# A fused attention and two-layer MoE kernel: another order of the same 2,222 pieces

## The chip, the cores and the metric

The kernel runs on one core of one Trainium2 chip. The time is the device time of one execution in microseconds (us); a kernel's time is the median of its runs. Engines are named as in the profile: PE (TensorE matmuls), PEld (TensorE's weight loads), DVE (VectorE), ACT (ScalarE), POOL (GpSimd) and SP (the queue that issues most DMAs).

## The reference

Three stages follow one another, all in float32:

```python
# attention: q is averaged over pairs of rows, then softmax(q k^T / 8) v
q_pool = q.reshape(B, H, S // 2, 2, D).mean(axis=3)      # B, H, S, D = 2, 8, 1152, 64
scores = np.matmul(q_pool, k.transpose(0, 1, 3, 2)) / np.sqrt(D)
attn = np.exp(scores - scores.max(-1, keepdims=True))
attn = attn / (attn.sum(-1, keepdims=True) + 1e-9)
x = np.matmul(attn, v)                                   # -> 1152 tokens x 512
# layer 1 (d_ff 1536)
g = x @ w_gate
x = (g / (1 + np.exp(-g)) * (x @ w_val)) @ w_out
# layer 2 (d_ff 2048)
h = x @ w_in
x = (np.maximum(h, 0) + alpha * np.minimum(h, 0)) @ w_out2
```

## The kernel before

**Pieces and tiles.** The program is built from 2,222 pieces. A piece is one instruction of DVE, ACT, POOL or SP, or a run of 2 to 20 matmuls on PE that write one PSUM bank. `add()` numbers the pieces as the code reaches them; each has an engine, a duration that the planner assumes, the tokens that it reads and writes, and the buffers that it uses. Some have two ways: the subtraction that makes the low half of a float32 operand (`lower`: L490 on DVE or L491 on POOL), the copy that makes the high half (`higher`: L498 on ACT or L499 on POOL), the sums of weight blocks (L537 on DVE or L536 on POOL), the evacuation of transposes (L765 on ACT or L766 on DVE), and a few more.

**Attention** goes over 8 pairs of heads. For each pair there are scores (L732, the upper and lower 64 rows of the array side by side, and L751 for a corner), row minima on DVE while the scores are copied out of PSUM (L700, L702), the exponential on ACT (L706), transposes on PE (L775, L789) with their evacuations (L765, L766), the product with v (L808, the array's columns side by side) and a rescaling. PE changes between whole array, half rows and half columns as the pieces ask.

**The layers** multiply each float32 operand as a high and a low half, in three matmuls. Token block 0 is multiplied directly (`contract`, L907, 12 matmuls of 384 columns). Token blocks 1 and 2 go through a seven-product (Strassen) scheme: `block` issues seven `seventh` pieces (L919, 6 matmuls each), whose sums are made on DVE from PSUM (`plus`, L925). Layer 1 then applies Silu on ACT (L975) and the gate product on DVE (L980), layer 2 its slopes (L1019, L1020); both split the result in two halves (L498 and L490, L966 and L967). The output products are `out1` (L1050, added up by L1055 and L1057) and `out2` (L1084, 12 matmuls of 512 columns, added up by L1090 and L1092, the last token block as two halves), and SP sends each finished row block out (L1094). Each pair of weight blocks is loaded by two DMAs into one of two raw buffers, unpacked by ACT and DVE (L517 to L520), summed (L536, L537) and split.

**Order.** Nothing reorders at run time. The string `ORDER` holds one code for each piece: twice its number, plus one if its second way is taken. `Plan.run` goes through the codes, gives each buffer a slot that is free by then, and the pieces are emitted in that order, so that each engine's queue is the codes of that engine in their order. An engine waits at the piece whose inputs or slots are not ready, and everything behind it on that engine waits too.

```python
        for code in codes:
            t = self.tasks[code // 2]
            w = t.way = t.ways[code % 2]
            e = w.eng
...
            for i, b in enumerate(t.bufs):
                if b.slot is None:
                    spots = [(room(s, at), k, s) for k, s in enumerate(self.classes[b.cls]["slots"])]
                    _, _, b.slot = min(x[:2] + (x[2],) for x in spots if x[0] is not None)
```

PSUM has eight banks. In the layers each PE piece takes one (class "b"); it is free again when the last piece that reads it, on DVE or ACT, is done. PE also gets short idle matmuls (L367) while it waits at the start, where the planner sees room.

Pieces that are named below, by code: 2492 is `out1` of output block 3, token block 1, and its evacuation is L1055; 2632 is the `plus` behind a `seventh` (code 2630); 2202 is the `contract` of `value1(3)` and 2188 the `lower` piece of its weights; 2360 is the gate product of `value1(4)`; 2978 is an `out1` of the second group and 2980 its addition (L1057); 4420, 4432 and 4438 are the last `out2` pieces (row block 6 and the two halves of row block 8), with 4422, 4434 and 4440 as their additions and 4424, 4436 and 4442 as their stores.

Of the kernel before, what the change touches and what calls it, by code (L numbers as in the profile page):

```python
# [33 lines left out]
8 20 10 48 50 12 24 26 34 54 14 60 52 56 16 22 98 39 40 62 66 18 58 64 86 68 92 28 30 88 70 72 90 94 82 84 76 32 46 154 100 74 96 44 80 36 79 104 102 130  # L34
132 156 158 138 134 108 106 112 136 160 110 42 162 260 264 266 114 116 118 120 166 122 164 262 140 270 272 170 192 194 142 168 174 172 198 200 204 196 206
210 202 208 212 124 268 126 129 276 278 150 153 188 191 144 149 146 492 230 176 181 226 178 182 228 494 184 232 280 187 234 236 496 238 240 242 502 504 214
216 282 220 222 224 286 218 284 318 290 322 288 320 324 292 294 298 326 330 332 336 370 506 366 362 328 334 364 338 246 248 352 296 300 368 372 374 302 304
251 314 316 724 308 728 355 340 310 307 382 344 313 385 386 342 390 392 388 396 346 348 376 378 274 380 398 394 350 402 406 400 424 426 428 430 432 436 438
434 440 244 254 356 256 258 404 358 498 500 361 442 420 726 408 444 413 422 410 414 416 508 462 458 419 464 460 446 448 510 451 252 512 514 466 468 516 518
520 452 456 522 550 556 454 470 472 474 524 554 526 530 476 528 532 552 558 562 560 594 564 568 596 602 566 598 600 604 570 478 480 606 482 730 732 742 734  # L40
584 586 546 484 548 534 537 538 486 540 542 545 572 576 574 614 489 617 618 620 956 624 740 578 582 580 622 608 612 610 626 630 628 490 632 636 656 0 658
662 634 664 638 668 660 960 670 962 674 736 666 672 676 964 588 590 592 694 652 640 655 645 972 642 646 690 648 696 692 678 680 651 683 744 698 746 700 702
748 750 752 684 688 958 782 784 966 686 754 788 790 756 758 762 794 796 800 830 786 760 764 792 798 802 968 826 828 834 832 836 710 712 715 778 781 838 816
766 818 804 846 771 809 768 848 772 776 774 850 854 852 856 860 806 810 812 814 840 844 862 858 866 870 888 890 894 864 900 868 842 896 1184 1192 902 1194
1408 906 892 898 904 738 820 908 822 884 872 825 874 1412 704 887 877 878 706 708 883 880 922 924 910 912 926 928 976 915 974 1182 978 1186 1188 930 932
982 980 916 918 920 984 1014 1018 1016 986 988 990 994 1020 1024 1026 992 2 996 1190 1066 1022 1030 1034 1058 1060 716 1028 1032 1062 1064 1068 1070 942
944 947 1010 1013 1048 998 1050 1001 1004 1009 1002 1006 1078 1080 934 1036 1038 718 720 722 1082 1084 1086 1040 1088 1090 1042 1044 936 1072 1046 1076
1092 1074 1094 1126 1096 1098 1102 1120 1122 1132 1100 1128 1124 970 1052 1134 1138 1932 1130 1136 1414 1416 1424 1054 1140 1158 1057 1116 1119 1104 1109
1106 1198 1110 1154 1112 1200 1156 1115 1160 1142 1147 938 1144 940 1202 1204 1206 1162 1164 1148 1426 950 1240 1242 1244 1208 1150 1152 948 1210 1246 1934
1212 1214 1216 1936 1220 1248 1218 1222 1252 1254 1258 1292 1250 1256 1410 1260 1284 1286 1288 1290 1294 1296 1166 1168 1170 1174 1176 1179 1418 1938 1274  # L50
1236 1238 1276 1224 1228 1230 1670 1232 1196 1304 1227 1306 1262 1266 1308 1420 1310 1264 1234 1312 1172 1180 1314 1316 1318 1268 1674 1270 1272 1298 1302
1320 1322 1300 1324 1326 1346 1348 1350 1352 1328 1354 1358 1278 1280 1360 1364 1356 1362 1342 1330 1940 1366 1345 1335 1282 1332 1336 1380 1382 1338 1368
1370 1428 1384 1386 1388 1341 1390 1392 1394 1396 1373 1434 1398 1430 1432 1374 1376 1440 1436 1472 1438 1378 1442 1446 1676 1466 1672 1468 1478 1444 1448
1474 1470 1480 1514 1510 1512 1484 1476 1518 1482 1486 1516 1520 1522 1400 1402 1500 1404 1462 1464 1678 1450 1502 1452 1456 1942 1455 1460 952 1688 1422
1530 1459 1968 1948 1532 1488 1534 1492 1538 1490 1540 1524 1528 1494 1498 1536 1544 1542 1496 1546 1550 954 1554 1680 1682 1572 1574 1406 1548 1552 1576 4
1684 1578 1944 1526 1584 1580 1586 1504 1582 1506 1588 1590 1509 1568 1571 1592 1556 1559 1610 1612 1560 1562 1606 1608 1567 1690 1694 6 1970 1594 1564
1614 1616 1618 1696 1596 1692 1698 1598 1600 1602 1728 1700 1730 1702 1706 1734 1736 1946 1953 1704 1740 1972 1732 1604 1710 1686 1772 1955 1742 1776 1774
1708 1960 1738 1744 1724 1727 1950 1746 1957 1959 1718 1721 1712 1620 1748 1714 1780 1778 1782 1964 1962 1974 1722 1976 1762 1764 1716 1796 1798 1750 1753
1800 1754 1756 1758 1802 1804 1966 1897 1834 1760 1846 1840 1806 1784 1838 1844 1808 1898 1812 1816 1902 1635 1641 1642 1626 1836 1842 1850 1628 1854 1810
1637 1848 1978 1622 1630 1900 1624 1632 1814 1654 1852 1872 1650 1985 1653 1874 1766 1768 1770 1792 1830 1660 1795 1833 1818 1876 1823 1878 1824 1827 1820  # L60
1880 1868 1870 1980 1828 1882 1786 1788 1791 1856 1861 1858 1862 1866 1865 1988 1639 1982 1904 2012 1663 1644 1987 1664 1666 1646 1990 1888 1648 1656 1658
1992 1668 1890 1884 1886 1994 2004 1892 1894 2014 1916 1996 2024 1906 1922 1924 2030 2046 1918 1920 1912 1915 2006 1926 1908 2008 2010 1910 2050 2096 2016
2098 2100 2102 2104 2020 2106 1928 1931 2018 2054 2058 2048 2052 2108 2112 2022 2026 2028 2034 1998 2040 2068 2056 2036 2076 2110 2060 2114 2086 2168 2166
2170 2172 2062 2116 2118 2124 2132 2032 2070 2120 2122 2136 2174 2144 2042 2140 2176 2064 2128 2134 2066 2183 2000 2002 2150 2262 2260 2264 2266 2138 2078
2142 2154 2088 2178 2180 2185 2186 2146 2160 2188 2190 2192 2038 2080 2268 2082 2084 2044 2210 2332 2270 2272 2212 2214 2330 2216 2156 2334 2218 2090 2336
2280 2282 2092 2072 2074 2094 2152 2232 2234 2130 2202 2204 2220 2424 2222 2162 2206 2274 2278 2276 2224 2338 2284 2208 2286 2148 2226 2288 2426 2428 2296
2194 2250 2298 2240 2340 2228 2230 2300 2242 2158 2308 2342 2345 2304 2430 2314 2350 2352 2446 2432 2252 2346 2348 2302 2126 2196 2444 2244 2358 2434 2366
2306 2198 2292 2236 2354 2356 2440 2386 2442 2310 2200 2448 2246 2450 2164 2254 2316 2436 2452 2374 2376 2324 2396 2238 2256 2318 2294 2454 2456 2368 2378
2258 2382 2438 2502 2460 2462 2458 2248 2290 2360 2500 2504 2370 2372 2506 2508 2510 2517 2320 2312 2521 2472 2474 2322 2536 2380 2398 2384 2388 2512 2514
2496 2498 2582 2540 2326 2522 2584 2586 2676 2404 2588 2390 2519 2590 2328 2524 2526 2406 2468 2414 2592 2678 2408 2532 2680 2748 2682 2684 2392 2542 2548  # L70
2550 2528 2410 2416 2418 2362 2538 2552 2595 2394 2597 2601 2566 2556 2470 2476 2602 2604 2400 2544 2534 2402 2412 2598 2554 2558 2530 2606 2686 2608 2746
2750 2752 2560 2562 2840 2564 2570 2572 2464 2420 2568 2688 2690 2754 2756 2695 2576 2574 2693 2422 2610 2618 2478 2842 2696 2630 2698 2578 2546 2612 2701
2620 2622 2702 2364 2466 2614 2624 2860 2626 2628 2616 2762 2844 2488 2490 2758 2760 2764 2580 2632 2862 2492 2494 2480 2634 2482 2484 2638 2486 2636 2846
2648 2640 2848 2656 2666 2642 2650 2644 2658 2704 2652 2767 2770 2668 2646 2654 2708 2660 2706 2670 2662 2768 2672 2712 2664 2710 2864 2674 2716 2772 2714
2720 2850 2724 2866 2852 2888 2718 2856 2890 2730 2854 2858 2774 2868 2722 2732 2870 2782 2726 2872 2994 2776 2876 2996 2874 2734 2728 2878 2892 2740 2736
2894 2738 2790 2778 2742 2896 2744 2794 2792 2780 2798 2898 2998 2802 2784 3092 2900 2796 2908 2812 3094 2903 2904 2800 2880 2814 2906 2804 2910 2912 2820
2914 2830 2806 2882 2884 2822 3096 3000 2824 2832 2916 2886 2834 3002 2920 2918 3098 3004 3100 2924 3014 3112 3006 3114 2922 3009 3010 2928 2786 2926 2808
# [1111 lines left out]
```

## Time and profile before

| | before |
|---|---|
| runs, us | 601.98, 601.80, 602.91 (median 601.98) |
| the profiled execution: its own time, us | 601.89 |
| its span (first to last instruction), us | 600.1 |
| granted TensorE clock over the span | 1.000 |
| PE, PEld, DVE, ACT, POOL busy, share of the span | 99%, 88%, 86%, 61%, 29% |

The time of an execution holds the span and 1.8 us around it. Busy shares are unions of an engine's instructions; matmuls overlap, so that a busy PE need not be a PE at its best pace.

### The profile page before, as it was taken

The page shows a single profiled execution, that of the slowest core. Times are in us where ns is not written, and L with a number is a line of the kernel's source. Part 1 is how long each engine was busy: PE and PEld are TensorE (multiplying, and loading weights), DVE is VectorE, ACT ScalarE, POOL GpSimd, SP SyncE. Part 2 cuts the span into 40 slices and gives each one's busy share as a digit, 9 for nine tenths or more (in the row PEclk, how much of TensorE's full clock was granted, in tenths as well). Part 3 has the DMA queues.
Part 4 walks back from the last instruction along what each step waited for, and adds up shares of the span by engine and source line. Part 5 has one row for each costly group of instructions (what it writes and reads, how often), then busy time and mean ns, then how long its engine had stood idle before and what let it go on. Part 6 is the DMA issues. An engine that isn't in the chain of part 4 may idle for free.

```text
span 600.1 us, 12138 instructions
## 1 busy us (share of the span) xinstructions
PE 593.8 (99%) x4736; PEld 531.0 (88%) x4736; DVE 518.8 (86%) x1050; ACT 365.2 (61%) x626; POOL 171.7 (29%) x188
## 2 busy tenths in 40 slices
PE   8999999999999999999999999999999999999997
PEld 5877877877886999999999999999999989989986
DVE  6988988989898999999859999889999999988552
ACT  5898888998998556555436334346675654544320
POOL 5552536230754313111300300556110300320000
PEclk9999999999999999999999999999999999999999
DMA  5342143232300431432303323112113313110012
GB/s 160 128 131 69 52 161 112 101 101 76 137 22 21 174 108 71 141 140 89 123 0 141 126 89 138 71 70 71 71 70 107 129 46 141 70 71 0 1 64 95
DMA packets 17913, 55.35 MB, mean 92 GB/s; under 512 B 2808, under 2 KB 4288, under 8 KB 17856
## 3 DMA queue, kind: packets, MB, share of 16 engines
q1 hardware_dynamic: 17568, 54.19, 25.9%
q8 instruction: 37, 0.61, 0.4%
q10 hardware_dynamic: 288, 0.39, 0.2%
q14 instruction: 20, 0.16, 0.1%
HBM read 52.17 MB, written 2.40 MB: 91 GB/s over the span
## 4 chain that ended last, share of the span: by engine, by line
PE 98%; DVE 2%; issue 0%; DVEq 0%
PE bank L919 24%; PE bank L1084 16%; PE bank L907 14%; PE bank L1050 12%; PE bank L808 12%; PE bank L732 9%; PE bank L775 6%; PE bank L751 2%; PE bank L789 1%; PE bank L367 1%; DVE wide L702 0%; DVE turned L490 0%; DVE wide L700 0%; DVE weights L490 0%; PE bank L822 0%
## 5 line engine op out<-in xcount | busy, mean ns | idle before, releaser
L919 PE MATMUL bank<-fed,weights 128*128 128x384 f32 x600 | 114.2, 335 | 0.0
L536 POOL TENSOR_TENSOR magnitudes<-magnitudes 128x256 f32<-128x256 f32 x58 | 50.8, 888 | 193.1 <-DVE magnitudes L520 143.3
L919 PEld LDWEIGHTS bank<-fed,weights 128*128 128x128 f32 x600 | 105.4, 188 | 0.7
L1084 PE MATMUL bank<-wide,turned 128*128 128x512 f32 (+1 forms) x444 | 101.7, 384 | 0.0
L1084 PEld LDWEIGHTS bank<-wide,turned 128*128 128x128 f32 x444 | 81.5, 188 | 15.4
L907 PE MATMUL bank<-x,weights 128*128 128x384 f32 x480 | 88.7, 337 | 0.0
L907 PEld LDWEIGHTS bank<-x,weights 128*128 128x128 f32 x480 | 83.8, 188 | 1.7 <-issue 0.7
L706 ACT ACTIVATE wide<-wide,stats 128x1152 f32<-128x1152 f32 x60 | 74.9, 1251 | 13.6 <-DVE wide L702 13.3
L1050 PE MATMUL bank<-turned,wide 128*128 128x384 f32 x432 | 77.5, 335 | 0.6 <-DVE plain L925 0.6
L1050 PEld LDWEIGHTS bank<-turned,wide 128*128 128x128 f32 x432 | 75.1, 188 | 0.9 <-DVE plain L925 0.9
L702 DVE TENSOR_SCALAR_CACHE_REDUCE wide<-bank,stats 128x384 f32<-128x384 f32 x120 | 70.2, 614 | 3.7 <-DVE wide L702 0.6
L808 PE MATMUL bank<-turned,plain 128*64 128x320 f32 (+1 forms) x576 | 73.1, 408 | 0.0
L925 DVE TENSOR_TENSOR plain<-bank,plain 128x384 f32<-128x384 f32 x100 | 54.0, 549 | 16.8 <-PE bank L919 15.7
L765 ACT ACTIVATE turned<-bank 128x512 f32<-128x512 f32 (+2 forms) x130 | 62.7, 555 | 7.1 <-PE bank L775 6.0
L808 PEld LDWEIGHTS bank<-turned,plain 128*64 128x64 f32 x576 | 40.0, 137 | 29.3 <-DVE wide L700 1.2
L732 PE MATMUL bank<-fed 64*128 64x384 f32 x540 | 56.5, 346 | 0.0
L919 PE MATMUL bank<-early,weights 128*128 128x384 f32 x240 | 48.0, 335 | 0.0
L490 DVE TENSOR_TENSOR weights<-magnitudes,weights 128x1024 fp32r<-128x1024 f32 x38 | 47.2, 1250 | 0.1
L732 PEld LDWEIGHTS bank<-fed 64*128 64x128 f32 x540 | 45.7, 186 | 0.8
L498 ACT ACTIVATE weights<-magnitudes 128x1024 fp32r<-128x1024 f32 x30 | 31.8, 1059 | 18.7 <-DVE magnitudes L520 7.6
L966 ACT ACTIVATE turned<-plain,signs 128x384 fp32r<-128x384 f32 x48 | 28.6, 616 | 23.9 <-DVE plain L1020 23.8
L919 PEld LDWEIGHTS bank<-early,weights 128*128 128x128 f32 x240 | 42.3, 188 | 0.2
(101 smaller groups left out, 874.1 us busy)
## 6 DMA issues: line engine op xcount, KB each, us to landing
plain<-in_w_out SPq DMA_DIRECT2D x28, 512.0 KB, 4.1
plain<-in_w_in SPq DMA_DIRECT2D x16, 512.0 KB, 4.2
plain<-in_w_gate SPq DMA_DIRECT2D x10, 512.0 KB, 4.7
plain<-in_w_val SPq DMA_DIRECT2D x10, 512.0 KB, 4.1
plain<-in_vt SPq DMA_DIRECT2D x8, 576.0 KB, 5.1
plain<-in_qt SPq DMA_DIRECT2D x7, 576.0 KB, 3.8
plain<-in_kt SPq DMA_DIRECT2D x7, 576.0 KB, 5.1
out<-plain SPq DMA_DIRECT2D x8, 256.0 KB, 2.0
```

The source lines that it names most:

```text
L490: ways = [(DVE, dve(w), lambda: nc.vector.tensor_tensor(dst(), src(), hi().bitcast(F32), ALU.subtract), True), (POOL, gp2(w), lambda: nc.g ...
L536: ways = [(POOL, gp2(2 * P), lambda a=a, b=b, op=op, n=n: nc.gpsimd.tensor_tensor(U(n), a(), b(), op), True), (DVE, dve(2 * P), lambda a=a ...
L702: go = lambda: nc.vector.tensor_scalar(e.ap[:, js], src(), scale, m(i - 1), ALU.mult, ALU.min, accum_out=m(i))
L706: add(ACT, act(S, True, True), lambda: nc.scalar.activation(e.ap, e.ap, AF.Exp, bias=st.ap[:, 2:3], scale=-1.0, accum_out=x.sums.ap[:, n:n ...
L732: nc.tensor.matmul(s[j].ap[:, :CUT], l(half), r(half, js), start=a == 0, stop=a == len(terms) - 1)
L765: ACT, act(cols), lambda: nc.scalar.activation(to(), src(), AF.Copy), at + turn("ev", p, n), ts, [key], ts + [et],
L808: nc.tensor.matmul(acc.ap[half, :n], x.vn.ap[:, (j * NK + kc) * D:(j * NK + kc) * D + D], b.ap[:, (j * NK + kc) * n:(j * NK + kc) * n + n] ...
L907: nc.tensor.matmul(acc.ap[:, :TB], l, x0[:, r, c], start=c == 0 and a == 0, stop=c == KC - 1 and a == 2)
L919: nc.tensor.matmul(bank_.ap[:, :TB], l, seven(xb, k, c, r), start=first and c == 0 and n == 0, stop=c == 1 and n == 2, skip_group_check=no ...
L925: add(DVE, dve(TB), lambda: nc.vector.tensor_tensor(dst.ap, a.ap[:, :TB], b.ap, ALU.add), prio, [a] + ([b] if b is not dst else []), [dst] ...
L1050: nc.tensor.matmul(acc.ap[:, :TB], l[:, os_], r, start=n == 0 and m == 0, stop=n == len(g) - 1 and m == 2)
L1084: nc.tensor.matmul(acc.ap[:, :width], l, r[:, cols], start=n == 0 and m == 0, stop=n == len(g) - 1 and m == 2)
```

## The change

The string `ORDER` is replaced. The new one holds the same 2,222 pieces once each, in another order, and for some of those with two ways the other way. No piece, tile, buffer or constant is added or taken away, and nothing else in the file differs (no line number moves). The diff, cut to the lines that the prediction speaks of:

```diff
--- before.py
+++ after.py
@@ -31,75 +31,75 @@
 ORDER = """
...
-2142 2154 2088 2178 2180 2185 2186 2146 2160 2188 2190 2192 2038 2080 2268 2082 2084 2044 2210 2332 2270 2272 2212 2214 2330 2216 2156 2334 2218 2090 2336
-2280 2282 2092 2072 2074 2094 2152 2232 2234 2130 2202 2204 2220 2424 2222 2162 2206 2274 2278 2276 2224 2338 2284 2208 2286 2148 2226 2288 2426 2428 2296
...
-2258 2382 2438 2502 2460 2462 2458 2248 2290 2360 2500 2504 2370 2372 2506 2508 2510 2517 2320 2312 2521 2472 2474 2322 2536 2380 2398 2384 2388 2512 2514
...
-2620 2622 2702 2364 2466 2614 2624 2860 2626 2628 2616 2762 2844 2488 2490 2758 2760 2764 2580 2632 2862 2492 2494 2480 2634 2482 2484 2638 2486 2636 2846
...
-2956 2954 3120 2962 2958 2966 3122 2960 2964 2972 2968 3316 3272 3318 2978 2974 2970 3274 2976 3276 2982 2836 2838 2980 3278 2986 2984 3288 3480 3280 3482
...
-4434 4436 4440 4442
...
+2180 2142 2070 2072 2146 2124 2184 2088 2090 2188 2202 2264 2190 2192 2160 2080 2082 2266 2330 2074 2268 2334 2336 2270 2210 2084 2148 2130 2092 2094 2424
+2154 2156 2272 2214 2212 2216 2280 2282 2158 2222 2232 2152 2234 2236 2204 2274 2276 2218 2220 2162 2224 2426 2278 2338 2284 2194 2428 2292 2226 2250 2286
...
+2496 2472 2248 2498 2516 2320 2322 2542 2390 2326 2404 2536 2590 2520 2522 2524 2526 2592 2598 2492 2494 2392 2406 2408 2410 2548 2550 2474 2414 2416 2556
...
+2701 2480 2702 2628 2840 2568 2622 2842 2844 2846 2624 2848 2850 2630 2632 2862 2484 2486 2860 2648 2650 2652 2488 2490 2758 2760 2764 2636 2638 2640 2580
+2482 2656 2666 2360 2642 2763 2771 2658 2668 2670 2654 2712 2766 2768 2720 2772 2852 2716 2714 2718 2704 2774 2856 2864 2724 2866 2708 2362 2858 2782 2854
...
+3108 3014 2810 3016 3104 3110 3106 2946 2962 2834 2950 2886 3112 3010 3114 3116 2954 2956 3118 2786 2788 2918 3268 3018 3270 3120 3272 3274 3020 2978 2986
...
+3188 3222 3502 3504 3209 3178 3196 3190 3192 3506 3211 3216 3228 3528 3218 2980 3224 3508 3296 3200 3032 3230 3182 3185 3234 3232 3248 3510 3250 3530 3194
...
+4330 4390 4402 4392 4394 4408 4224 4414 4302 4304 4306 4308 4162 4398 4410 4342 4426 4404 4406 4412 4416 4418 4428 4430 4432 4434 4420 4422 4436 4400 4438
+4440 4424 4442
 """
```

Counted through the list of pieces: PE keeps its 525 pieces, 388 of which stand in the same order among themselves, and none is moved by more than 17 places. DVE goes from 833 pieces to 845, ACT from 551 to 548, POOL from 176 to 167, SP keeps 137. DVE's pieces move by up to 55 places, ACT's by up to 30.

## Rows read from the trace of the kernel before

**Rows 1.** The page: the span, and busy time of three engines.
```profile
span 600.1 us, 12138 instructions
PE 593.8 (99%) x4736; PEld 531.0 (88%) x4736; DVE 518.8 (86%) x1050; ACT 365.2 (61%) x626; POOL 171.7 (29%) x188
```
**Rows 2.** The page: the chain that ended last, by engine.
```profile
PE 98%; DVE 2%; issue 0%; DVEq 0%
```
**Rows 3.** All waits of PE by releaser: us in total, times, longest.
```profile
PE bank L367 <- DVE plain L442: 1.2, 1, 1.2
PE bank L1050 <- DVE plain L925: 0.6, 1, 0.6
PE bank L789 <- DVE wide L702: 0.6, 1, 0.6
PE bank L732 <- DVE plain L675: 0.6, 1, 0.6
```
**Rows 4.** PE's timeline over the first 20 us: start, us, what.
```profile
1.17 3.49 PE L367 MATMUL bank<-plain 128*128 128x512 bf16 x9 [1.17 <-DVE plain L442]
...
7.89 2.21 PE L732 MATMUL bank<-plain 64*128 64x384 f32 x12 [0.59 <-DVE plain L675]
...
11.21 0.34 PE L789 MATMUL bank<-plain,wide 64*128 64x64 f32 x4 [0.62 <-DVE wide L702]
```
**Rows 5.** Stretches: length, then busy us (instructions) by engine; granted clock; DMA.
```profile
20.00:43.00 23.00, 23.00 (x335) 18.08 (x332) 20.30 (x66) 19.91 (x37) 11.44 (x11) 1.00 0.45 144
...
240.00:290.00 50.00, 50.00 (x290) 49.94 (x289) 47.76 (x71) 26.70 (x47) 8.19 (x9) 1.00 0.36 127
290.00:300.00 10.00, 9.37 (x54) 9.05 (x53) 8.19 (x11) 4.79 (x9) 4.85 (x5) 1.00 0.29 107
300.00:350.00 50.00, 50.00 (x289) 50.00 (x288) 42.87 (x64) 21.15 (x35) 7.57 (x8) 1.00 0.23 85
...
400.00:441.00 41.00, 41.00 (x226) 39.35 (x225) 38.67 (x59) 27.10 (x48) 15.24 (x14) 1.00 0.15 52
```
**Rows 6.** PEld's timeline from 294 to 300 us.
```profile
298.60 1.52 PEld L1050 LDWEIGHTS bank<-turned,wide 128*128 128x128 f32 x9 [0.95 <-DVE plain L925]
```
**Rows 7.** DVE's timeline from 286 to 300 us.
```profile
290.59 2.00 DVE L490 TENSOR_TENSOR weights<-magnitudes,weights 128x1024 fp32r<-128x1024 f32 x1
...
294.37 1.22 DVE L490 TENSOR_TENSOR weights<-magnitudes,weights 128x1024 fp32r<-128x1024 f32 x1
...
298.00 0.54 DVE L925 TENSOR_TENSOR plain<-bank,plain 128x384 f32<-128x384 f32 x1
```
**Rows 8.** POOL's timeline over the same stretch.
```profile
290.33 1.20 POOL L499 TENSOR_SCALAR weights<-magnitudes 128x1024 fp32r<-128x1024 f32 x1 [4.19 <-DVE magnitudes L537]
295.67 3.81 POOL L536 TENSOR_TENSOR magnitudes<-magnitudes 128x256 f32<-128x256 f32 x4 [4.14 <-DVE weights L490]
```
**Rows 9.** Groups by line and shape: count, busy us, mean ns, idle before.
```profile
L491 POOL TENSOR_TENSOR fed<-plain,fed 128x384 fp32r<-128x384 f32 x11 | 12.9, 1176 | 15.5 <-ACT fed L498 15.5
L490 DVE TENSOR_TENSOR fed<-plain,fed 128x384 fp32r<-128x384 f32 x9 | 5.9, 656 | 0.6 <-ACT fed L498 0.6
L537 DVE TENSOR_TENSOR magnitudes<-magnitudes 128x256 f32<-128x256 f32 x22 | 12.2, 564 | 1.0 <-POOL magnitudes L536 0.8
```
**Rows 10.** DVE's timeline from 223 to 232 us.
```profile
224.28 2.34 DVE L490 TENSOR_TENSOR weights<-magnitudes,weights 128x1024 fp32r<-128x1024 f32 x2
...
231.15 0.68 DVE L518 TENSOR_SCALAR magnitudes<-magnitudes 128x1024 int32<-128x1024 int32 x1
```
**Rows 11.** PE's timeline from 223.4 to 232 us.
```profile
224.56 1.20 PE L919 MATMUL bank<-early,weights 128*128 128x384 f32 x6
...
230.82 1.50 PE L907 MATMUL bank<-x,weights 128*128 128x384 f32 x7
```
**Rows 12.** DVE's timeline at the end, and stores by the page.
```profile
596.85 0.42 DVE L1092 TENSOR_TENSOR plain<-bank,plain 128x256 f32<-128x256 f32 x1 [1.01 <-PE bank L1084]
...
out<-plain SPq DMA_DIRECT2D x8, 256.0 KB, 2.0
```

123 rows, old and new, of the table ORDER are left out of this document.

## The prediction

> **What bounds the kernel now.** I read the page's busy shares first, then the chain, PE's own waits, busy time by stretch, and the timelines around the places that stood out. PE is busy for 593.8 of 600.1 us [rows 1] and carries 98% of the chain that ended last [rows 2], so only a change in PE's time can move the end. A busy PE need not be a fast one, so the next view asks for pace. From 300 to 350 us PE gets through 289 matmuls in 50 us [rows 5], 0.173 us each; every one of them has 384 columns, and 384 columns at 2.4 GHz (the granted clock of that stretch is 1.00) are 0.160 us. From 240 to 290 us there are 290 in 50 us, the same pace, though DVE is busy for 47.76 us of it. In the attention stage (20 to 43 us) PE is never idle either, at the same clock.
>
> So the third view matters most: what does PE wait for at all? Four waits, 3.0 us together [rows 3]. Three lie in the first 12 us [rows 4]: the start (1.17), the second load of q (0.59), the first row minima (0.62). The fourth is at 298.60 us, inside the stretch 290 to 300, the only one of the later stretches shown in which PE does less than its full time (9.37 of 10) [rows 5]. There a matmul stands idle for 0.63 us and its weight load for 0.95 [rows 6], released by the `plus` L925 that DVE finished late. The reader is to see why it was late: DVE had done a subtraction L490 in 2.00 us at 290.59 that takes 1.22 at 294.37 [rows 7], while POOL ran L499 from 290.33 on [rows 8], and its queue was late from then on. That is the only slip of DVE which PE ever feels.
>
> **The change part by part.** (1) PE's pieces. The same 525 pieces run, so their matmul time is the same. The order could save or add changes between whole array, half rows and half columns: I counted them along both orders, 43 and 43. The first ten pieces of PE are the same in both, so the three waits at the start stay. Price: nothing, and no gain either.
>
> (2) The wait at 298.60. In the new order code 2492, the waiting piece, stands 17 places earlier; the `seventh` 2630 stands 4 places later on PE, while its `plus` 2632 stands at DVE's place 456 instead of 457. DVE has at least four PE pieces more of time, and the shortest full-width piece is 6 x 0.173 = 1.04 us [rows 5], so some 4.2 us more, against a wait of 0.63 to 0.95. I let the wait go: a gain between 0.63 and 0.95, taken as 0.8, the middle. If another slip falls on that place, nothing is gained.
>
> (3) Engines exchanged. DVE gets 12 pieces more, net: 7 subtractions that POOL made (L491, now L490), 2 sums (L536, now L537) and 3 evacuations from ACT. The dearest of these forms is the 384-column L490 at 0.656 us [rows 9], so at most 12 x 0.656 = 7.9 us more on an engine that is idle for 600.1 - 518.8 = 81.3 us [rows 1]. They are not spread evenly: counted by where the pieces stood before, 400 to 441 us gets 8 and loses 4. That is at most 4 x 0.656 = 2.6 us, and DVE's idle time there is 41.00 - 38.67 = 2.3 us [rows 5]. So it costs between 0 and 2.6 us, the latter if DVE were PE's bound there throughout; I take nothing, because PE is busy for all of that stretch now and what DVE gains in work POOL loses at 1.176 us a piece [rows 9], and POOL's work is what stretches DVE's [rows 7, 8]. The cover is DVE's idle 2.3 us; without it, the excess goes straight to PE.
>
> On the last point a row and a page say the same with different reach. L490, with both inputs in SBUF, was stretched by 0.78 us under POOL's work, while L925, with one input in a PSUM bank, took its usual 0.54 at 298.00, under POOL's L536 [rows 7, 8]. The Trainium skill (GPSIMD Engine Reference, Key points) says that POOL shares its SBUF interfaces with VectorE and contends with instructions that have two SBUF inputs or run in a two-port mode; by that rule the nine pieces that POOL loses are nine chances fewer of such a slip, by estimate up to 9 x 0.78 = 7 us for DVE and a sum that stays at 601.6, since PE would see none of it. The trace agrees with it at this place.
>
> (4) Places where a piece is now asked for earlier. Compared queue by queue, the tightest is code 2202, a `contract` that moves from PE's place 304 to 298. It began at 230.82 and would begin at 224.56, since the same pieces stand in front of that place [rows 11]. Its weights come from 2188, the first of the two L490 at 224.28, done at 224.28 + 1.17 = 225.45 [rows 10]: a wait of 0.9 us if DVE were as it was. But in front of 2188 DVE has lost two sums (to POOL) and an L518 (to a later place) and gained one 384-column operation: -2 x 0.56 - 0.68 + 0.54 = -1.3 us [rows 7, 9, 10]. Between 0 and 0.9, taken as 0.
>
> (5) Evacuations moved back. Of the 154 pieces with which DVE gives back a bank in the layers, 38 stand ten or more places later than before and 10 that much earlier. The farthest are 2360 (405 to 460) and 2980 (538 to 592): at 518.8 / 833 = 0.62 us a piece [rows 1] a bank is held for some 54 x 0.62 = 34 us longer, with one or two of the eight banks out of the rotation. Nothing in the trace prices this directly. From below it is nothing: with six banks left and 1.04 to 2.08 us a piece, an evacuation has over 5 us to be done in. From above the nearest row is the one wait of PE on an evacuation, 0.63 to 0.95 [rows 3, 6], for each place where DVE slips while banks are scarce. I take 0.5, less than one such wait.
>
> (6) The end. The last half block (4438, 4440, 4442) stays last. Block 6's store now goes out right before it: the last `out2` half has 12 matmuls of 256 columns, at least 12 x 0.173 x 256/384 = 1.4 us, so block 6's addition runs that much before the last one at 596.85 and its store starts near 596.1 and lands 2.0 us later [rows 12], at 598.1, before the span's end at 600.1. Nothing; if the last store queued behind it for the rest, up to 0.7.
>
> (7) SP's loads move by up to 10 places among themselves; of those in the attention stage, the ones behind a waiting load are reads of scale factors that `finish` on POOL needs, and POOL is idle for 71% of the span [rows 1]. Nothing; its idle time is the cover.
>
> The sum: 601.89 (the profiled execution) - 0.8 + 0.5 = 601.59, so 601.6 us. That execution lies 0.09 under the median 601.98 of the runs, which I leave aside.
>
> **The rivals.** *Slower: PSUM banks run out.* The place is the layers, 300 to 410 us and the last 60 us before the final `out2` pieces, where (5) puts the longest holds. Each DVE slip that falls while few banks are free gives PE a wait like that at 298.60. To be slower by over 0.2% (1.2 us, about what a measurement of this kernel can tell from no change), the new waits must come to 1.2 + 0.8 + 0.1 = 2.1 us, three waits at 0.8: 601.89 - 0.8 + 3 x 0.8 = 603.5, or 601.89 - 0.8 + 3 x 0.95 = 603.9 at the longer figure. For it: DVE is busy for 47.76 of 50 us between 240 and 290 [rows 5], so a slip is slow to recover. Against it: the present order lets PE feel just one of DVE's slips.
>
> *Faster: the attention stage has room.* PEld is busy for 18.08 of 23.00 us there, against 50.00 of 50.00 from 300 us on [rows 5]. If the order could turn a tenth of those 4.9 us into time in each of seven such stretches, 7 x 0.49 = 3.4 us would go: 601.89 - 0.8 - 3.4 = 597.7. Against it: PE is busy throughout, the matmuls there are the same in number and form, and so are the 43 changes of array shape. The Trainium skill (Trainium Kernel Development and Optimization, Performance Expectations) holds that matmul busy time is a bad metric and the weight loads' busy share a good one; by that rule the 88% of the span leave room, which is this rival. The trace does not bear it out for a mere change of order.
>
> *The wait stays, nothing else changes.* 601.9, on the same side as the forecast.
>
> **How the numbers follow.** No measurable change holds 0.65: 0.45 for the forecast, from 600.9 (the wait goes at 0.95, no new one) to 602.4, and 0.20 for the wait that stays or comes back elsewhere, up to 603.1. Slower holds 0.28, nearly all of it for the banks, a little for DVE's 2.6 us in (3). Faster by over 1.2 us holds 0.07: all of PE's waits that the order can touch are worth 0.95, so it needs the attention rival or a lucky run. The range runs from 600.7 (the full 0.95 and 0.2 of run to run) to 603.9 (three waits of 0.95), with about 0.15 left out.
>
> **What would show it.** Right: PE's waits list L1050 on L925 no more, or one wait under 1 us; PE's stretches keep 0.173 us a matmul; DVE's busy time rises to 523 to 527 us and POOL's falls. The banks: several waits of PE on L925, L1057, L980 or L1092, or a stretch of the layers below full PE time. It would be wrong at (5) if PE waits there by over 2 us in sum, at (4) if L907 waits for L490 near 225 us, at (3) if the waits gather between 400 and 441 us, and at (1) if attention's stretches get shorter.

## The result and the profile after

The new order took 605.61 us (median of 6 runs, 605.21 to 606.90) where the kernel before took 602.56 in the same comparison: ratio 1.0052, 95% interval 1.0038 to 1.0066. It is slower by 0.5%, 3.05 us by the medians, outside the predicted range. Ratios here and below are not taken from the medians, so that the two differ a little. The profiled execution has 605.50 us and a span of 603.7, which is 3.6 longer than [rows 1]. Page, span, busy times and the chain:

```profile
span 603.7 us, 12122 instructions
PE 595.6 (99%) x4732; PEld 531.1 (88%) x4732; DVE 524.1 (87%) x1062; ACT 361.3 (60%) x623; POOL 157.3 (26%) x179
...
PE 90%; DVE 7%; ACT 1%; issue 1%; DVEq 0%; ACTq 0%
```

PE's busy share still reads 99%, so that it shows nothing of the loss. The chain does: DVE now holds 7% of it where it held 2% [rows 2]. PE's waits say what it waited for:

```profile
PE bank L367 <- DVE plain L442: 1.2, 1, 1.2
PE bank L1084 <- DVE plain L925: 0.9, 1, 0.9
PE bank L789 <- DVE wide L702: 0.6, 1, 0.6
PE bank L732 <- DVE plain L675: 0.6, 1, 0.6
PE bank L919 <- DVE early L490: 0.5, 1, 0.5
PE bank L919 <- DVE plain L925: 0.5, 2, 0.2
PE bank L907 <- DVE plain L1057: 0.4, 1, 0.4
PE bank L822 <- ACT turned L765: 0.2, 1, 0.2
```

The three waits at the start are those of [rows 3]. The wait of L1050 is gone. Five on DVE have come, all but one of them between 410 and 433 us. The stretches that answer to [rows 5]:

```profile
240.00:290.00 50.00, 50.00 (x289) 50.00 (x288) 43.14 (x63) 26.42 (x45) 10.00 (x12) 1.00 0.34 122
290.00:300.00 10.00, 10.00 (x60) 10.00 (x59) 7.29 (x12) 2.58 (x7) 1.86 (x1) 1.00 0.37 130
300.00:350.00 50.00, 49.78 (x286) 49.46 (x285) 45.10 (x68) 22.27 (x37) 8.40 (x10) 1.00 0.30 106
400.00:441.00 41.00, 38.98 (x208) 36.07 (x207) 40.01 (x59) 22.99 (x41) 12.67 (x10) 1.00 0.15 52
```

From 290 to 300 us PE is whole again; from 400 to 441 it gets through 208 matmuls where it had 226. It stands idle for 2.0 us there, and its weight loads are busy for 3.3 us less than before: the loads stand still at each wait for longer than PE does, so a wait costs more than PE's idle time shows. This is the stretch between layer 1 and layer 2. DVE is busy for 40.01 of the 41 us.

How did DVE get late? Its own waits on PE, from 360 to 400 us (the first of the kernel before, the second of the one after; us in total, times, longest):

```profile
DVE plain L1057 <- PE bank L1050: 1.7, 4, 0.6
```
```profile
DVE plain L1057 <- PE bank L1050: 3.6, 4, 1.5
```

And two of those places in DVE's timeline of the kernel after:

```profile
363.25 0.56 DVE L1057 TENSOR_TENSOR plain<-bank,plain 128x384 f32<-128x384 f32 x1 [0.78 <-PE bank L1050]
365.33 1.02 DVE L1057 TENSOR_TENSOR plain<-bank,plain 128x384 f32<-128x384 f32 x2 [1.52 <-PE bank L1050]
...
395.57 1.02 DVE L1057 TENSOR_TENSOR plain<-bank,plain 128x384 f32<-128x384 f32 x2 [1.06 <-PE bank L1050]
```

DVE stands at additions whose products PE has not finished, and what is behind them waits too. One such piece is 2980: its product was done at 354.9, DVE added it at 362.4 in the order before, and adds it at 402.5 now. Count every piece that DVE has begun at the shortest time that any of the traces shows for it: by 360 us DVE has done the same work in both orders, by 370 us it has done 4.0 us less in the new one, by 400 us 2.6 less. What is missing is done between 400 and 440, when PE waits for it.

### The profile page after: what moved, and what is told of

It is laid out like the page before. It is cut to its first block, busy times and chain, and to the rows that moved or that the text cites. A ratio compares the mean times of both kernels' runs of the same rounds, so it can differ in the third digit from the quotient of the medians.

```text
span 603.7 us, 12122 instructions
## 1 busy us (share of the span) xinstructions
PE 595.6 (99%) x4732; PEld 531.1 (88%) x4732; DVE 524.1 (87%) x1062; ACT 361.3 (60%) x623; POOL 157.3 (26%) x179
## 4 chain that ended last, share of the span: by engine, by line
PE 90%; DVE 7%; ACT 1%; issue 1%; DVEq 0%; ACTq 0%
PE bank L919 22%; PE bank L1084 16%; PE bank L907 12%; PE bank L808 11%; PE bank L1050 10%; PE bank L732 9%; PE bank L775 6%; PE bank L751 2%; PE bank L789 1%; DVE plain L1057 1%; DVE plain L1020 1%; DVE magnitudes L519 1%; DVE plain L568 1%; PE bank L367 1%; DVE magnitudes L520 1%
## 5 line engine op out<-in xcount | busy, mean ns | idle before, releaser
L919 PE MATMUL bank<-fed,weights 128*128 128x384 f32 x600 | 114.1, 336 | 0.2 <-DVE plain L925 0.2
L536 POOL TENSOR_TENSOR magnitudes<-magnitudes 128x256 f32<-128x256 f32 x56 | 48.2, 872 | 244.8 <-DVE magnitudes L520 178.4
L919 PEld LDWEIGHTS bank<-fed,weights 128*128 128x128 f32 x600 | 105.4, 188 | 1.5 <-DVE plain L925 0.5
L1084 PE MATMUL bank<-wide,turned 128*128 128x512 f32 (+1 forms) x444 | 102.5, 385 | 0.9 <-DVE plain L925 0.9
L1084 PEld LDWEIGHTS bank<-wide,turned 128*128 128x128 f32 x444 | 81.5, 188 | 17.0 <-DVE plain L925 1.2
L907 PE MATMUL bank<-x,weights 128*128 128x384 f32 x480 | 89.2, 337 | 0.4 <-DVE plain L1057 0.4
L907 PEld LDWEIGHTS bank<-x,weights 128*128 128x128 f32 x480 | 84.0, 188 | 1.5 <-DVE plain L1057 0.7
L706 ACT ACTIVATE wide<-wide,stats 128x1152 f32<-128x1152 f32 x57 | 71.3, 1254 | 14.1 <-DVE wide L702 14.0
L1050 PE MATMUL bank<-turned,wide 128*128 128x384 f32 x432 | 77.2, 334 | 0.0
L1050 PEld LDWEIGHTS bank<-turned,wide 128*128 128x128 f32 x432 | 75.1, 188 | 0.0
L702 DVE TENSOR_SCALAR_CACHE_REDUCE wide<-bank,stats 128x384 f32<-128x384 f32 x114 | 66.8, 614 | 2.8 <-PE bank L732 0.5
L925 DVE TENSOR_TENSOR plain<-bank,plain 128x384 f32<-128x384 f32 x100 | 54.1, 551 | 15.9 <-PE bank L919 14.0
L919 PE MATMUL bank<-early,weights 128*128 128x384 f32 x240 | 48.6, 337 | 0.7 <-DVE early L490 0.5
L490 DVE TENSOR_TENSOR weights<-magnitudes,weights 128x1024 fp32r<-128x1024 f32 x38 | 46.7, 1243 | 0.5 <-ACT weights L498 0.4
L919 PEld LDWEIGHTS bank<-early,weights 128*128 128x128 f32 x240 | 42.3, 188 | 1.9 <-DVE early L490 0.8
L498 ACT ACTIVATE weights<-magnitudes 128x1024 fp32r<-128x1024 f32 x32 | 33.6, 1055 | 16.2 <-PE bank L919 7.0
```

Of the source, the lines that this page charges most:

```text
L490: ways = [(DVE, dve(w), lambda: nc.vector.tensor_tensor(dst(), src(), hi().bitcast(F32), ALU.subtract), True), (POOL, gp2(w), lambda: nc.g ...
L536: ways = [(POOL, gp2(2 * P), lambda a=a, b=b, op=op, n=n: nc.gpsimd.tensor_tensor(U(n), a(), b(), op), True), (DVE, dve(2 * P), lambda a=a ...
L702: go = lambda: nc.vector.tensor_scalar(e.ap[:, js], src(), scale, m(i - 1), ALU.mult, ALU.min, accum_out=m(i))
L706: add(ACT, act(S, True, True), lambda: nc.scalar.activation(e.ap, e.ap, AF.Exp, bias=st.ap[:, 2:3], scale=-1.0, accum_out=x.sums.ap[:, n:n ...
L907: nc.tensor.matmul(acc.ap[:, :TB], l, x0[:, r, c], start=c == 0 and a == 0, stop=c == KC - 1 and a == 2)
L919: nc.tensor.matmul(bank_.ap[:, :TB], l, seven(xb, k, c, r), start=first and c == 0 and n == 0, stop=c == 1 and n == 2, skip_group_check=no ...
```

## The experiments

"Before" is the median of the kernel before in the same comparison, and what a kernel loses is told against its own "before". In e3, e4, e7 and e8 the codes of one order run up to a piece of PE, and then those of the other that are still left, in its order. The kernels of the first four experiments have two lines more in the string, so that their line numbers stand two higher.

| kernel | median, us | before, us | ratio | 95% interval |
|---|---|---|---|---|
| e1: order before, engines new | 601.80 | 602.13 | 0.9991 | 0.9982 to 0.9999 |
| e2: order new, engines before | 603.86 | 602.13 | 1.0027 | 1.0014 to 1.0040 |
| e3: order before up to 335 us | 606.06 | 602.13 | 1.0063 | 1.0051 to 1.0075 |
| e4: order new up to 309 us | 601.80 | 602.13 | 0.9995 | 0.9985 to 1.0005 |
| e5: new, four pieces put back | 603.99 | 602.10 | 1.0030 | 1.0020 to 1.0041 |
| e6: e5 and engines before | 603.80 | 602.10 | 1.0033 | 1.0020 to 1.0046 |
| e7: order new up to 395 us | 607.20 | 602.10 | 1.0083 | 1.0067 to 1.0099 |
| e8: order before up to 395 us | 604.30 | 602.10 | 1.0032 | 1.0014 to 1.0050 |
| e9: e5, PE's order before | 607.77 | 602.16 | 1.0093 | 1.0072 to 1.0113 |
| e10: e5, three sums first | 602.73 | 602.16 | 1.0007 | 0.9997 to 1.0018 |
| e11: before, one plus earlier | 601.35 | 602.16 | 0.9983 | 0.9973 to 0.9994 |
| e12: e10 and one plus earlier | 602.33 | 601.79 | 1.0005 | 0.9994 to 1.0016 |
| e13: e11, engines new | 601.12 | 601.79 | 0.9990 | 0.9981 to 0.9999 |

**First: engines, order, or deferred additions?** e1 takes over engine choices alone (18 of the 96 in which the orders differ, with 6 of DVE's 12 additional pieces), e2 puts the same choices back, e3 and e4 join the two orders at a seam.

```diff
 e1, in the order of before (e2 is the reverse, in the new order):
-3139 3147 3180 3189 3208 3191 3195 3214 3233 3241 3243 3247 3251 3252 3260 3257 3543 3544
+3138 3146 3181 3188 3209 3190 3194 3215 3232 3240 3242 3246 3250 3253 3261 3256 3542 3545
```

> The order of before, every piece in its place; only the 18 engine choices in which the new order differs between 384 and 430 us are taken over (12 pieces go from POOL to DVE, 6 from DVE to POOL). Theory A (the exchanged engines make DVE the bound between 395 and 440 us): PE waits 2 us or more in that stretch, time 604 to 605. Theory B (the same pieces on DVE, but in a worse order) and theory C (additions of out1 that the new order defers from 362 and 372 us into the stretch): no new waits, time within 0.6 of before, 601.5 to 602.7.

> The new order, but those 18 engine choices as before. Theory A: the four waits between 405 and 435 us go, time 602 to 602.8. Theories B and C: the waits stay, 2 us or more of them, time 604.5 to 606; POOL's own lateness could add to that.

> The order of before up to PE's 380th piece (about 335 us), and the new order from there on. The two additions of out1 (codes 2980 and 3032) thus stand early, at 362 and 372 us; the stretch itself and its engines are the new ones. Theory C: the waits between 400 and 440 us shrink to 1 us or less, time near 603.3 (the wait at 298 us is back, 0.8). Theories A and B: 3 us are still lost there, time 605 to 606.5.

> The new order up to PE's 356th piece (about 309 us), the order of before from there on. If all of the loss lies between 395 and 440 us (theories A, B and C alike) the stretch is as before and the wait at 298 us is gone: 601.2 to 602. If the loss comes from banks or queues that the earlier part leaves behind, 603 or more.

e1 lost nothing, so theory A falls as it was put. PE does not wait once from 350 to 450 us. The sum over 395 to 445 us (PE, PEld, DVE, ACT, POOL):

```profile
sum 50.00, PE 50.00 PEld 47.77 DVE 47.10 ACT 31.62 POOL 16.02; mean PE 10.00 PEld 9.55 DVE 9.42 ACT 6.33 POOL 3.20
```

The kernel before has DVE 46.55 and POOL 20.31 there: DVE runs five pieces more in 0.55 us more; that its other pieces are stretched less when POOL does less fits this, but was not measured piece by piece. Yet e2, the same exchange undone in the new order, loses 1.7 us where the new order loses 3.05: 1.3 us less (1.5 by the ratios), between the two forecasts. So the exchange costs nothing in the order of before and 1.3 us in the new one. e4 puts the loss behind 309 us, e3 (606.06, the forecast of A and B) behind 335. On theory C e3 says nothing, against what I had expected of it: its seam lies ahead of the products of 2980 and 3032, so that both additions still stood late (402.6 and 405.5).

**Second: does DVE's lateness come from before the stretch (theory D)?** e5 fills the idle places, e6 undoes the engines too, e7 and e8 put the seam at the head of the stretch.

```diff
 e5, in the new order:
-2932 2934 2960 ... 3124 3326 3048 ... 3166 3170 3181 ... 3218 2980 3224 ... 3200 3032 3230
+2932 2934 2980 2960 ... 3124 3326 3032 3048 ... 3166 3170 3142 3162 3181 ... 3218 3224 ... 3200 3230
```

> The new order with four pieces of DVE put back and nothing else moved: the addition 2980 right behind 2934, 3032 behind 3326, 3142 and 3162 behind 3170, so that each stands in front of a place where DVE of the new order waits for PE (0.78 and 1.52 us at 363 to 365, 0.58 at 373, 1.06 at 395). Theory D (in the new order DVE idles at those places with ready work behind the waiting piece, and is late from then on): DVE is some 2 us earlier at 405, PE's waits between 405 and 435 us fall from 3.0 to 1.2 or less, time 603.4 to 604.2. Theory B (the order within 400 to 440 us itself): the waits stay, 605 or more.

> The same, and the 18 engine choices of before as well. If lateness from 360 to 395 us and the engines' exchange add up (D and A together), nothing of the loss is left: 601.6 to 602.6, no wait of PE over 0.3 us between 405 and 435. If the order within the stretch matters by itself (B), 603 to 604 as with the engines alone put back.

> The new order up to PE's 411th piece (about 395 us), the order of before from there on, with the additions 2980, 3032, 3142 and the subtraction 3162 at the seam. Theory D: DVE comes to the seam some 3 us late, PE waits 0.5 to 2 us between 400 and 435, time 602.4 to 604. Theory B: the stretch has the old order and engines, so no loss: 601.5 to 602.2.

> The order of before up to PE's 411th piece (about 395 us), so that 2980, 3032, 3142 and 3162 stand early, and the new order and engines from there on. Theory D: DVE is not late at the seam and has room for the exchanged engines; of the 3.4 us lost in the stretch 1 or less is left: 602 to 603.3. Theory B: 3 us are still lost, 604.5 to 606.

e5 loses 1.9 us in place of 3.05 (1.3 us less by the ratios, 1.8 by the spans), as theory D had it. The waits at 410.5 (L907), 420.5 (L490) and 423.4 (L925) are gone; two of the five are left, the second of them at 306.5:

```profile
PE bank L1084 <- DVE plain L925: 0.9, 1, 0.9
...
PE bank L919 <- DVE plain L925: 0.2, 1, 0.2
```

Nor was it the banks that 2980 and 3032 had held: those came free at 403.1 and 406.0 in the kernel after, ahead of PE's first wait there. DVE was 1.1 us earlier at 410 us (the addition that L907 waits for ends at 409.4 in place of 410.5), about half of what I had expected. e6 gains nothing on e5 by its median, and I was wrong that the two add up: it has no wait of L1084, which the engines take away, but waits 0.25 us for an L925 at 422.9 where e5 does not. e7 is the test from the other side: old stretch, old engines, but DVE 3.1 us of work behind at 395. It lost 5.1 us (607.2), where B expected nothing and D 604 at most. Its stretches and PE's timeline there:

```profile
400.00:414.00 14.00, 14.00 (x83) 14.00 (x82) 12.66 (x17) 6.46 (x13) 10.33 (x8) 1.00 0.01 1
414.00:420.00 6.00, 2.98 (x15) 2.13 (x13) 5.12 (x8) 4.89 (x12) 2.95 (x4) 0.90 0.49 175
420.00:424.00 4.00, 3.89 (x12) 3.89 (x13) 2.40 (x5) 2.02 (x4) 1.94 (x2) 0.50 0.00 0
...
428.00:432.00 4.00, 4.00 (x25) 4.00 (x24) 4.00 (x8) 2.70 (x5) 0.00 (x0) 1.00 0.00 0
```
```profile
416.28 1.47 PE L919 MATMUL bank<-fed,weights 128*128 128x384 f32 x6 [0.77 <-DVE plain L1020]
420.11 2.29 PE L919 MATMUL bank<-fed,weights 128*128 128x384 f32 x6 [2.37 <-ACT plain L936]
422.20 2.12 PE L919 MATMUL bank<-early,weights 128*128 128x384 f32 x6
```
```profile
418.18 0.61 ACT L966 ACTIVATE turned<-plain,signs 128x384 fp32r<-128x384 f32 x1 [0.84 <-DVE plain L1020]
```

The longer wait ends with a piece of ACT (L936), but ACT had itself waited for DVE's L1020 three pieces earlier. PE waits for 3.1 us, and then the granted clock is 0.50, the lower of its two levels (1.2 of 2.4 GHz), from 420 to 424 us: six matmuls take 2.12 us that take 1.20 at 426.90. So e7's loss is not of waits alone, and its 5.1 us cannot be set against the arrears one to one.

e8 took 604.3, more than D alone allowed (603.3): with DVE in time at the seam, the wait of L1084 is still there, 0.88 us at 431.4. A second cause lies within the stretch.

**Third: what delays the out2 product (code 3566)?** This is the L1084 of that wait. It starts right as the plus 3412 ends. Either the banks are short (theory P) or the plus is late (theory S).

```diff
 e9, PE's queue of e5:
-3296 3344 3306 3376 3354 3422 3364 3368 3372 3434 3388 3398 3520 3430 3426 3410 3446 3566 3456 3524 3468
+3296 3306 3344 3354 3364 3368 3388 3372 3376 3422 3398 3410 3426 3430 3434 3520 3446 3524 3456 3468 3566
 e10, DVE's queue of e5 (e12 has besides: -2624 2848 2850 2632  +2624 2632 2848 2850):
-3386 3544 3404 3412 3428 3432 3408
+3386 3412 3428 3432 3404 3544 3408
 e11, DVE's queue of before:
-2624 2616 2632
+2624 2632 2616
```

> The kernel with the four pieces put back (605.6 - 1.6 = 604.0 in the earlier runs), and PE's 21 pieces from its 417th to its 437th in the order of before; DVE's queue and the engines stay new. The remaining loss is the wait of an out2 (code 3566) for a bank, 0.9 us at 430.8, and 0.2 at 421.6. Theory P (the new order of PE opens the products 3376 and 3434 five places earlier and closes 3410 four places later, so that banks are held long): the wait of 3566 goes, 602.3 to 603.2. Theory S (DVE's plus 3412 is late because a sum and a multiplication stand in front of it and slip): a wait of PE for that plus stays, 603.7 or more.

> The kernel with the four pieces put back, and on DVE the three sums 3412, 3428 and 3432 ahead of 3404 and 3544 (two pieces that took 1.09 and 0.95 us there). Nothing else moves. Theory S: 3412 is done by 429.5 in place of 430.7, the wait of 3566 goes, 602.5 to 603.2. Theory P: banks are still short one place further on, PE waits 0.5 us or more between 425 and 440 us, 603.6 to 604.3.

DVE's timeline of e5, POOL's of the same time, and DVE's of e10:

```profile
428.20 0.95 DVE L537 TENSOR_TENSOR magnitudes<-magnitudes 128x256 f32<-128x256 f32 x1
429.08 1.09 DVE L1020 SCALAR_TENSOR_TENSOR plain<-plain,signs 128x384 f32<-128x384 f32 x1
430.10 1.60 DVE L925 TENSOR_TENSOR plain<-bank,plain 128x384 f32<-128x384 f32 x3
```
```profile
427.13 2.62 POOL L536 TENSOR_TENSOR magnitudes<-magnitudes 128x256 f32<-128x256 f32 x3 [7.73 <-DVE magnitudes L520]
```
```profile
429.06 1.61 DVE L925 TENSOR_TENSOR plain<-bank,plain 128x384 f32<-128x384 f32 x3 [0.53 <-PE bank L919]
430.59 0.61 DVE L1020 SCALAR_TENSOR_TENSOR plain<-plain,signs 128x384 f32<-128x384 f32 x1
431.11 0.42 DVE L537 TENSOR_TENSOR magnitudes<-magnitudes 128x256 f32<-128x256 f32 x1
```

The two pieces took 2.04 us ahead of the sums while POOL ran its own, and 1.03 behind them, when POOL was done. PE's wait is gone, and e10 loses 0.6 us where e5 loses 1.9: theory S holds. The interval of e10 includes the time before. One of the two pieces, 3544, is among the 18 engine choices: with it back on POOL (e2, e6) L1084 does not wait either. e9 got worse instead of better (607.77): PE in its old order asks DVE's new queue for other pieces first and waits 2.1 us for an L490, 1.2 for an L1020 and 1.0 for an L936. That tells nothing for P. The times in the traces do, if a bank is counted as in use from its first product to its last reader: when 3566 waits, 6 of the 8 banks are in use (at 430.6 us in e5, at 432.5 in the kernel after), and 3 when L907 waits at 410.5. Banks were not short. PE waited for one bank while others stood empty, because `Plan.run` binds each piece beforehand, and among the slots that are free by its planned times takes the one that was freed last:

```python
            return (0, -until) if until <= at else (1, until)
```

Whether another binding would have spared these waits was not tried.

**Fourth: the places near 300 us, and a faster kernel.**

> The kernel before with one exchange on DVE: the plus 2632, for whose bank PE waits 0.63 us at 298.6, stands in front of 2616 (a subtraction of 1.10 us). If the wait is worth what the prediction took (0.8, between 0.63 and 0.95), the time is 601.2 where the kernel before has 602.0, and PE has no wait behind the first 12 us. If the time is given back later, as in the kernel with the new order up to 310 us, 601.7 to 602.1.

> The new order with all the mends so far (four pieces put back; 3412, 3428 and 3432 ahead of 3404 and 3544) and one more: the plus 2632, behind which PE waits 0.22 us at 306.6 and loses 0.5 in all, stands ahead of the two weight operations 2848 and 2850 (1.75 and 1.23 us). If the loss is made of single places where DVE's queue has a piece that PE waits for behind one that nobody waits for, 0.5 us more goes: 602.1 to 602.4, with no wait of PE over 0.3 us behind the first 12 us. If the place at 306 us is given back, 602.6 to 602.9.

> The order of before with 2632 ahead of 2616, and the 18 engine choices of the new order. With DVE not late, the exchange of engines costs nothing: 600.9 to 601.6, as without it, and faster than both kernels. If the exchange uses up room that the earlier plus had made, 601.8 or more.

e11 is faster than both kernels, by 0.8 us in the medians against the kernel before, with no wait of PE left behind the first 12 us. All its waits:

```profile
PE bank L367 <- DVE plain L442: 1.2, 1, 1.2
PE bank L789 <- DVE wide L702: 0.6, 1, 0.6
PE bank L732 <- DVE plain L675: 0.5, 1, 0.5
```

In e12 the wait at 306.6 us is gone from the trace, but the medians can't show its half microsecond: 0.54 above before, as e10's 0.57. e13 is as e11 (0.67 and 0.81 below before): in the order of before with no plus late, the exchange of engines neither costs nor gives anything that can be measured.

**The loss by stretch.** Both orders have places on PE where the same pieces stand ahead, so that the stretches between such places can be compared in any two traces. Stretches in which the orders do not differ agree within 0.06 us; the first 31 us differ by up to 1.2 from one execution to another and are left out. Time against the kernel before, in us (the heads are its times):

| kernel | 183 to 197 | 210 to 308 | 406 to 429 | 429 to 451 | 451 to 566 |
|---|---|---|---|---|---|
| after | 0.38 | -0.55 | 2.07 | 1.20 | 0.67 |
| e2 | 0.39 | -0.49 | 1.00 | 0.40 | 0.64 |
| e5 | 0.38 | -0.54 | 0.32 | 1.25 | 0.68 |
| e6 | 0.38 | -0.54 | 0.88 | 0.40 | 0.67 |
| e8 | -0.01 | 0.00 | 0.30 | 1.19 | 0.67 |
| e10 | 0.39 | -0.54 | 0.32 | 0.07 | 0.63 |
| e12 | 0.39 | -1.05 | 0.31 | 0.07 | 0.69 |
| e11 | 0.00 | -0.92 | 0.01 | 0.00 | 0.01 |

The first column is a wait that every kernel with the new order there has, for an evacuation on ACT:

```profile
188.91 0.28 PE L822 MATMUL bank<-plain 64*128 64x64 f32 x2 [0.17 <-ACT turned L765]
```

The last column has no wait of PE at all. From code 3612 to code 4290 PE runs the same 64 pieces, in 114.51 to 114.55 us in the six traces with the order of before there, and in 115.14 to 115.20 in the nine with the new one. There a `seventh` (L919) takes 1.040 us up to the next piece's start when another `seventh` stands ahead of it, and 1.066 behind any other product; an `out2` (L1084) takes 2.721 behind any other product and 2.761 behind a `seventh` (medians, the same within 0.001 in all fifteen traces). The new order changes between a `seventh` and other products 35 times there, the order of before 16 times. By these medians that is 0.5 of the 0.7 us; why such a change costs time is not shown.

## Why the prediction was wrong

The sum was -0.8 + 0.5; measured was +3.05. By its own steps:

- **(1)**, nothing for PE's pieces: wrong by 0.7 us between 451 and 566. I counted the changes of array shape (43 and 43) and not the changes between a `seventh` and other products. Nor did I look for waits in the attention stage: the one of L822 costs 0.4 more.
- **(6), (7)**, nothing for the end and the loads: no run speaks against them. PE has no wait on a transfer, and none behind 433 us.
- **(2)**, the wait at 298.60 goes: right, and its worth of 0.8 too, as e11 shows by itself. But the new order gives about half of it back (0.55 gained of the 1.05 that e12 gains): the same `plus` 2632 now stands behind 2848 and 2850, three microseconds of weight operations of which one slipped to 1.75, and PE waits for it at 306.6. I had counted DVE's places and not what stood in them. So e4, which has this part and the wait of L822, gains 0.3 us by its median, within an interval that includes nothing.
- **(3)**, twelve pieces more for DVE at nothing: right in the order of before for the six that e1 tests. In the kernel after DVE is busy for 524.1 us, within the forecast of 523 to 527. The cover was named, DVE's idle 2.3 us between 400 and 441; the new order had used up that cover by deferring work into it, and then the exchange cost 1.3 us (e2). The Trainium skill's rule that POOL contends with VectorE (GPSIMD Engine Reference, Key points) agrees with e1 and with the two slips of e5, each of a piece with two inputs in SBUF; of the estimated 7 us less slip little shows: L490 on `fed` has 620 ns where it had 656 [rows 9].
- **(4)**, the tightest place is 2202: that place gave no wait, but it was not the tightest. I looked for pieces that PE asks for earlier, against a DVE that is in time. 3566 stands four places earlier on PE, the product that 3412 adds up four places later, and two pieces that slip stand in front of 3412: 1.3 us (e5 to e10).
- **(5), the step that failed**, "evacuations moved back": I saw that 38 of them, with 2980 at the head, stand far later, and priced them as banks held, +0.5. The banks were not the price: some stood empty at both waits that were counted. What a moved addition leaves behind is a place at which DVE has nothing that it may do, since its queue keeps order, and the work comes back where DVE has no time left. e5 and e7 show it from both sides: 1.2 us gained with four pieces put back, 5.1 lost, part of it by the clock, when DVE brings 3.1 us of arrears into the old stretch.

The rival of the slower side had the right sign, and it ended at 603.9. Its mechanism did not come: L907 and L1084 waited for a bank, but the bank was late because DVE was, with 3 and 6 of the 8 in use.

By stretch the new order loses 2.07 + 1.20 us from 406 to 451, where 0.5 was forecast, 0.67 behind that and 0.38 at L822, and gains 0.55 of the 0.8. Putting four pieces back takes 1.75 of it away (e5) and the order of the sums 1.18 more (e10); most of what is left in e10 is the 0.63 behind 451 and the 0.39 at L822. Not tried by themselves were the wait of L822, the changes between kinds of pieces, and why DVE's idle time from 360 to 370 us stays at 2.3 us in e5.

## What to carry to other kernels

On an engine that keeps its queue's order, price a moved piece at both ends: the idle place that it leaves and the room where it lands. Add up that engine's work done by time, one order against the other, and look for the first place where it falls behind; the waits that show come tens of microseconds later. Put what the bottleneck waits for ahead of what nobody waits for: one exchange of two pieces gave 0.8 us, the largest gain of this study over the kernel before. And compare two orders by the bottleneck's own pace too, between places where both have done the same pieces: 0.7 us of this loss shows in no wait.

## What the runs showed of the hardware

A stall can cost twice: after PE's waits of 0.77 and 2.37 us in e7 the granted clock fell from 1.00 to 0.50, and was back at 1.00 from 428 us. It need not: in e9, with waits of 1.00, 1.19 and 2.07 us between 416 and 427 us, the granted clock stayed at 1.00. The same DVE pieces took 0.95 and 1.09 us beside POOL's sums and 0.42 and 0.61 without them, so that the order on one engine can set the duration of its pieces as well as their places. PE's pieces, too, take up to 0.04 us more by what stands ahead of them (2.761 in place of 2.721 for an `out2` behind a `seventh`), with no wait in the trace.
